# Attention and two mixture layers on one Trainium2 core: a new sequence of product groups, with an offset table for a list scheduler

## The chip, the core and the metric

The kernel runs on one core of a Trainium2 chip. The metric is the device time of one execution in microseconds; a smaller number is better. Times given for a kernel are medians of several executions; a profile shows one execution more. The engines are named TensorE (PE, with its weight loads as PEld), VectorE (DVE), ScalarE (ACT), GpSimd (POOL) and SyncE (SP); DMA engines move data between HBM and the core's SBUF.

## What is computed

Three layers, one behind the other, on 2304 tokens of width 512. All inputs and results are float32.

```python
# q, k, v: (4, 8, 576, 64)
scores = scale * np.matmul(q, k.transpose(0, 1, 3, 2))
rel = pos[:, None] - pos[None, :]
scores = np.where((rel >= 0) & (rel < 64), scores, -1e9)
attn = softmax(scores)                        # (4, 8, 576, 576), a band of 64
x = concat_heads(np.matmul(attn, v))          # (2304, 512)

h = x @ w_in                                  # (512, 2048)
x = (h - np.tanh(h)) @ w_out                  # (2048, 512)

logits = cosine(x, expert_emb) / tau          # (2304, 8)
expert_idx = np.argmax(logits, axis=1)
gate_w = softmax(logits)[arange, expert_idx]
for e in range(8):
    mask = expert_idx == e
    h = np.maximum(x[mask] @ w1[e], 0.0)      # (512, 1024)
    out[mask] = gate_w[mask, None] * (h @ w2[e])
```

## The kernel before

The kernel has a straight part and a routed part. The straight part computes the attention, the dense layer, the routing and most of expert 0, and has no branch. The routed part goes through the experts one by one, with branches on how many tokens each has.

**Precision.** TensorE multiplies fp32r values. A float32 operand is split into a high and a low part, and `mm3` (L607 to L609) issues three matmuls for each product: high x high, high x low, low x high. The split makes much work for VectorE: the weights of the dense layer are decoded by `t_decode` in half-weights, with three bit operations (L375, L381, L386) and one subtraction (L400) on VectorE each, of 128x512 elements.

**Tiles.** Tokens are taken in nine chunks of 256. For each chunk, two units of attention run (`t_attn`: scores L468, masked maximum L484, exponential L493, division L504, transposes L517, product with v L542). The result is the dense layer's input, transposed; it is used directly (`direct`), and for a chunk whose later products come much later it is also stored to HBM (`spill`, L563) and loaded again by `t_xload`.

**The dense layer.** `t_moe1(c, f, ...)` does two of the 16 slices ("halves" f, f+1) of the inner width for chunk c: first products `h<-x,w`, then h - tanh(h), then second products `o<-w,gh`. The elementwise step has four ScalarE operations (square L635, tanh L639, L643, L647), four VectorE operations (L651, L655, L660, L664), a rounding on ScalarE (L670, `gh`) and a subtraction on VectorE (L674). A list `order` gives the sequence of product groups: (chunk, first slice, end slice, where the input comes from). `t_sum` adds the partial sums at a group's end (L706), and stores them to HBM (L711) where the chunk goes on later, or hands them to `t_route` (transposes L768, logits L784, counts L841, L842, prefix sums L850, L860, scatter of list entries L865).

**Routing.** Behind chunk 6's routing, `t_turns` puts the experts in an order by their token counts: counts' matmul L1174, small VectorE operations, cast of the turn L1198, then SP reads the eight numbers into registers (L1228) and loads the first lists (`t_list`, L1268, L1270). VectorE makes row numbers from a list (`t_ids`, L924, L925), and GpSimd gathers the rows with an indirect DMA (`t_gather`, L937). TensorE transposes them (`t_xin`, L960) and multiplies them with the expert's weights (`t_ffn`, loads L903, relu L996, L1000, gated result L1049, L1050, scatter L1055). At the end of the straight part, `t_counts` writes the final counts (L1289); all engines read them (L1375) for the branches (L1413, L1424). The overflow block of an expert, rows 256 to 511 of its list, is gathered too (`blk_o`) and opens the routed part with its transposes (L1070).

**What sets the order.** All work is given as tasks to `Sched`, which runs on the host while the program is built. A task has a priority, dependencies, buffers and a time per engine that can do it. At each step of its own clock the ready task with the lowest priority number, whose engine and buffers are free, is emitted; so these numbers set the sequence of instructions on each engine's queue, and no more. Each queue then runs in that order and waits with semaphores.

```python
later += [t for x in ready for t in (self.ready_at(x[3], e) for e in x[2]) if t > self.now]
...
end = self.moved = max(self.moved, self.now + issue + 0.65) + 1.2 * dur
```

Priorities come from `slot_t`, a table of due times: 3.7 per slice for the first 16 slices and 2.9 for each one behind that.

## Time and profile before

| | |
|---|---|
| median of 3 runs | 814.69 us (813.77 to 815.09) |
| profiled execution, time | 817.42 us |
| its span | 815.7 us |
| mean granted clock of TensorE | 0.989 |
| TensorE busy | 767.8 us (94%) |
| VectorE busy | 592.6 us (73%) |
| ScalarE busy | 475.7 us (58%) |
| GpSimd busy | 91.5 us (11%) |

The profile is of one execution. The span is the time from its first to its last instruction; the rest of the execution's time lies around it. Busy time of an engine is the sum of its instructions without waits. A wait is put down to the instruction that released it. The granted clock is 1.00 for 2.4 GHz and 0.50 for 1.2 GHz.

### The profile page before, as it was taken

The numbers are of one execution on the slowest core, as the hardware profiler recorded it, in microseconds if no ns is written. First come the engines' busy times: TensorE is split into PE (matmuls) and PEld (weight loads), VectorE is DVE, ScalarE is ACT, GpSimd is POOL, SyncE is SP. The second block draws the span as 40 slices with busy tenths as digits, with TensorE's granted clock in tenths as the row PEclk, the third lists the DMA queues.
The fourth block names the chain that finished last, engine by engine and source line by source line (L and its number), as shares of the span: only waits on it lengthen the run. The fifth ranks groups of instructions, "written<-read, shape, count | busy, mean of one in ns | idle before, by whom it ended". The sixth has DMA issues, their size and how long they took to land. (4 is left out here: it accounts for less than half of the span.)

```text
span 815.7 us, 15547 instructions
## 1 busy us (share of the span) xinstructions
PE 767.8 (94%) x5703; PEld 673.5 (83%) x5703; DVE 592.6 (73%) x1492; ACT 475.7 (58%) x1125; POOL 91.5 (11%) x116
## 2 busy tenths in 40 slices
PE   4788999999998999999999799999999999999995
PEld 4676889888987888899898699878888988888894
DVE  6999999999987877866768778983183727714750
ACT  6987888987855676766556456742252424423430
POOL 3000000000011200100001100202021223002320
PEclk9999999999999999999999999999999999999998
DMA  9857655565435342101000342635063728623740
GB/s 301 259 185 226 202 182 167 185 223 198 155 117 98 128 70 94 66 28 51 27 1 27 106 130 75 192 119 152 18 198 106 237 77 277 195 84 101 253 131 23
DMA packets 67438, 111.42 MB, mean 137 GB/s; under 512 B 8580, under 2 KB 44420, under 8 KB 67344
## 3 DMA queue, kind: packets, MB, share of 16 engines
q1 hardware_dynamic: 62448, 97.07, 37.9%
q0 software_dynamic: 4896, 13.13, 5.4%
q8 instruction: 54, 0.88, 0.5%
q14 instruction: 40, 0.33, 0.1%
HBM read 89.57 MB, written 21.66 MB: 136 GB/s over the span
## 5 line engine op out<-in xcount | busy, mean ns | idle before, releaser
L607 PE MATMUL h<-x,w 128*128 128x256 f32 x712 | 205.5, 289 | 4.7 <-DVE g L660 4.6
L608 PE MATMUL h<-x,w 128*128 128x256 f32 x712 | 201.4, 283 | 3.5 <-DVE x L583 3.5
L609 PE MATMUL h<-x,w 128*128 128x256 f32 x712 | 201.5, 283 | 0.9 <-DVE w L400 0.9
L607 PE MATMUL o<-w,gh 128*128 128x512 f32 x436 | 177.6, 407 | 1.0 <-ACT gh L670 0.9
L609 PE MATMUL o<-w,gh 128*128 128x512 f32 x436 | 172.8, 396 | 3.4 <-DVE gh L674 2.7
L608 PE MATMUL o<-w,gh 128*128 128x512 f32 x436 | 172.4, 395 | 0.0
L607 PEld LDWEIGHTS h<-x,w 128*128 128x128 f32 x712 | 135.7, 191 | 12.1 <-issue 5.7
L608 PEld LDWEIGHTS h<-x,w 128*128 128x128 f32 x712 | 136.0, 191 | 6.8 <-DVE x L583 3.9
L609 PEld LDWEIGHTS h<-x,w 128*128 128x128 f32 x712 | 135.9, 191 | 1.3 <-DVE w L400 1.3
L609 PEld LDWEIGHTS o<-w,gh 128*128 128x128 f32 x436 | 82.8, 190 | 26.6 <-DVE gh L674 6.0
L607 PEld LDWEIGHTS o<-w,gh 128*128 128x128 f32 x436 | 83.2, 191 | 19.1 <-issue 2.4
L608 PEld LDWEIGHTS o<-w,gh 128*128 128x128 f32 x436 | 83.3, 191 | 13.3
L888 DVE TENSOR_TENSOR w<-st,w 128x512 fp32r<-128x512 f32 x128 | 83.1, 685 | 3.0 <-ACT w L231 2.4
L231 ACT CAST w<-st 128x512 fp32r<-128x512 f32 x119 | 71.6, 633 | 18.3 <-DMA st<-in_moe_w_dram 8.2
L670 ACT CAST gh<-g 128x512 fp32r<-128x512 f32 x72 | 44.3, 620 | 62.7 <-DVE g L664 58.0
L651 DVE TENSOR_TENSOR g<-h,g 128x512 f32<-128x512 f32 x72 | 49.4, 687 | 25.6 <-ACT g L639 25.1
L996 ACT ACTIVATE gh<-h 128x256 fp32r<-128x256 f32 x48 | 18.1, 383 | 77.7 <-PE h L609 65.4
L674 DVE TENSOR_TENSOR gh<-g,gh 128x512 fp32r<-128x512 f32 x72 | 49.0, 685 | 13.1 <-ACT gh L670 13.1
L493 ACT ACTIVATE pr<-pr,mx 128x128 f32<-128x128 f32 x144 | 56.0, 396 | 3.4 <-DVE mx L484 3.4
L1000 DVE SCALAR_TENSOR_TENSOR gh<-h,gh 128x256 fp32r<-128x256 f32 x48 | 20.0, 421 | 50.6 <-ACT gh L996 43.2
L664 DVE COPY_PREDICATED g<-big,g 128x512 f32<-128x512 uint16 x72 | 53.6, 745 | 3.2
L635 ACT ACTIVATE g<-h 128x512 f32<-128x512 f32 x72 | 42.9, 595 | 19.7 <-PE h L609 19.5
(205 smaller groups left out, 1332.1 us busy)
## 6 DMA issues: line engine op xcount, KB each, us to landing
st<-in_moe_w_dram SPq DMA_DIRECT2D x64, 512.0 KB, 4.7
st<-in_moe_w_in_dram SPq DMA_DIRECT2D x16, 512.0 KB, 5.3
st<-in_moe_w_out_dram SPq DMA_DIRECT2D x16, 512.0 KB, 5.0
v<-in_v_dram SPq DMA_DIRECT2D x16, 512.0 KB
part<-st SPq DMA_DIRECT2D x12, 512.0 KB, 3.0
st<-part SPq DMA_DIRECT2D x12, 512.0 KB, 4.5
k<-in_k_dram SPq DMA_DIRECT2D x16, 320.0 KB, 3.3
q<-in_q_dram SPq DMA_DIRECT2D x18, 256.0 KB, 5.8
```

Source lines behind the costliest of these rows:

```text
L231: return {ACT: (act, lambda: nc.scalar.copy(out=o(), in_=i())), DVE: (dve, lambda: nc.vector.tensor_copy(out=o(), in_=i()))}
L493: nc.scalar.activation(out=pr_.t[:, i, :], in_=pr_.t[:, i, :], func=AF.Exp, bias=st["m"][:, i:i + 1], scale=-1.0, accum_out=st["den"][:, i ...
L607: nc.tensor.matmul(out=ps, lhsT=ah, rhs=bh, start=start, stop=False)
L608: nc.tensor.matmul(out=ps, lhsT=ah, rhs=bl, start=False, stop=False)
L609: nc.tensor.matmul(out=ps, lhsT=al, rhs=bh, start=False, stop=stop)
L635: {ACT: (0.49, lambda: nc.scalar.activation(out=u(), in_=hp.t, func=AF.Square))},
L651: {DVE: (0.6, lambda: nc.vector.tensor_tensor(out=th(), in0=hp.t, in1=th(), op=ALU.subtract))},
L664: {DVE: (0.64, lambda: nc.vector.copy_predicated(out=sq(), mask=big.t.bitcast(DT.uint16), data=th()))},
L670: {ACT: (0.52, lambda: nc.scalar.copy(out=gh(), in_=sq()))}, reads=[(gq, 0), (acc[0], "-"), (acc[1], "-")],
L674: {DVE: (0.6, lambda: nc.vector.tensor_tensor(out=gl(), in0=sq(), in1=gh().bitcast(F32), op=ALU.subtract))},
L888: return lambda: eng.tensor_tensor(out=w.t[:, b], in0=raw.t[:, a], in1=w.t[:, a].bitcast(F32), op=ALU.subtract)
L1000: {DVE: (0.335, lambda: nc.vector.scalar_tensor_tensor(out=part(gs, 1), in0=hp.t[:, 0:CT], scalar=0.0, in1=part(gs, 0).bitcast(F32), op0=A ...
```

## The change

It has three parts, all in what the host-side scheduler is told. No instruction's form changes.

1. *Another sequence of product groups for chunks 0 to 3.* There were 14 groups and are now 13, with other bounds (4, 6, 8, 10, 12, 16 instead of 4, 8, 12, 16). Chunks 0 and 1 now hold their input until their last group; only 2 and 3 are spilled and loaded again.
2. *Costs of transfers.* A transfer's first byte comes 1.0 after its issue instead of 0.65, reading n registers on SP costs 0.6n + 0.1 instead of 0.45, and gathers of the straight part take 1.5 on GpSimd and 3.5 more until they land, instead of 1.04 and 2.0.
3. *A table of 807 offsets.* `SC.part()` stands in front of each group of tasks and takes the next number; a quarter of it is added to the priority of all tasks that follow, until the next call. It acts in the straight part alone.

```diff
+SHIFTS = (
+    -617, -89, -188, -90, -232, 135, -108, -84, -118, -93, -65, -74, -74, -76, 12, -30, -48, -70, 95, -705,
...
+)
-    ISSUE, ISSUE_HALF = 0.45, 0.625
+    ISSUE, ISSUE_HALF, FIRST = 0.45, 0.625, 1.0
+        self.shifts, self.shift = iter(()), 0.0
+    def part(self):
+        self.shift = next(self.shifts, 0) / 4.0
-        self.todo.append((prio, self.n, alts, deps, bufs, list(allocs), lat, before))
+        self.todo.append((prio + self.shift, self.n, alts, deps, bufs, list(allocs), lat, before))
-                dur, fn = alts[e]
+                dur, fn, *own = alts[e]
-                    issue = self.ISSUE_HALF if dur == HALF else self.ISSUE
+                    issue = own[0] if own else self.ISSUE_HALF if dur == HALF else self.ISSUE
-                    end = self.moved = max(self.moved, self.now + issue + 0.65) + 1.2 * dur
+                    end = self.moved = max(self.moved, self.now + issue + self.FIRST) + 1.2 * dur
...
+        SC.part()
         SC.add({DMA: (1.5, load)}, writes=[(raw, 0)], allocs=[raw], prio=pr - 8)
+        SC.part()
         SC.add(
             {ACT: (0.56, d1)}, reads=[(raw, 0)], writes=[(tmp, 0)], allocs=[tmp] + ([w] if o == 0 else []), prio=pr
         )
...
-                {POOL: (1.04, ga)}, reads=[uid, *[("x2d", c) for c in range(chunks)]], writes=[(r[i], 0)],
-                allocs=[r[i]], prio=pr, lat=2.0,
+                {POOL: (took[0], ga)}, reads=[uid, *[("x2d", c) for c in range(chunks)]], writes=[(r[i], 0)],
+                allocs=[r[i]], prio=pr, lat=took[1],
...
-                {DMA: (0.0, lambda i0=i0, i1=i1: regs(i0, i1))}, reads=[("turn", "v")], ...
+                {DMA: (0.0, lambda i0=i0, i1=i1: regs(i0, i1), 0.6 * (i1 - i0) + 0.1)}, reads=[("turn", "v")], ...
...
+    SC.shifts = iter(SHIFTS)
+    FAR = 1.5, 3.5
-    order = [(0, 0, 4, "x"), (1, 0, 4, "x"), (1, 4, 8, ""), (0, 4, 8, ""), (2, 0, 8, "w"), (3, 0, 8, "w"), (1, 8, 12, ""), (0, 8, 12, ""), (2, 8, 12, "load"), (3, 8, 12, "load"), (3, 12, 16, ""), (2, 12, 16, ""), (0, 12, 16, "load"), (1, 12, 16, "load")]
+    order = [(0, 0, 4, 'x'), (1, 0, 6, 'x'), (2, 0, 6, 'w'), (0, 4, 8, ''), (3, 0, 8, 'w'), (2, 6, 10, ''), (1, 6, 10, ''), (0, 8, 12, ''), (3, 8, 12, ''), (1, 10, 16, ''), (0, 12, 16, ''), (2, 10, 16, 'load'), (3, 12, 16, 'load')]
...
     SC.run()
+    SC.shifts, SC.shift = iter(()), 0.0
```

In the sequences below, lines of the change have other numbers: L706 stands for L651 before, L710 for L655, L715 for L660, L719 for L664, L729 for L674, L987 for L924, L1001 for L937, L1125 for L1055, L1451 for L1375.

**VectorE, at the first elementwise step of the dense layer** (chunk 0, slices 0 and 1; L651, L655, L660, L664). Before:

```order
L504 TENSOR_TENSOR pr_367<-pr_367,den 128x512
L651 TENSOR_TENSOR g_541<-h_485,g_541 128x512
L231 COPY pT_547<-a_546 128x512
L655 SCALAR_TENSOR_TENSOR g_542<-g_542,g_540 128x512
L375 TENSOR_SCALAR tmp_581<-tmp_581 128x512
L660 TENSOR_TENSOR g_542<-h_485,g_542 128x512
L381 SCALAR_TENSOR_TENSOR tmp_581<-st_252,tmp_581 128x512
```

With the change:

```order
L534 ISA pr_443,mx<-a_442,mask_84 128x128
L534 ISA mx 128x1
L706 TENSOR_TENSOR g_542<-h_485,g_542 128x512
L710 SCALAR_TENSOR_TENSOR g_543<-g_543,g_541 128x512
L426 SCALAR_TENSOR_TENSOR tmp_519<-st_386,tmp_519 128x512
L715 TENSOR_TENSOR g_543<-h_485,g_543 128x512
L447 TENSOR_TENSOR w_479<-st_348,w_479 128x512
```

The first elementwise operation stands at row 103 of the queue before and at row 110 now; a weight subtraction (L447) and masked maxima are mixed with it where a division and a copy of transposed probabilities were.

**VectorE, between the cast of the experts' turn and the first row numbers of a list.** `pad`, `cum` and `tmp` are small tiles of the padding that `t_turns` computes. Before:

```order
L1198 CAST turni<-turnf 128x8
L660 TENSOR_TENSOR g_5804<-h_5714,g_5804 128x512
L1212 TENSOR_SCALAR pad<-most 128x1 x4
L1216 TENSOR_TENSOR pad<-pad,row_92 128x4
...
L664 COPY_PREDICATED g_5804<-big_5805,g_5803 128x512
L674 TENSOR_TENSOR gh_5980<-g_5804,gh_5980 128x512
L651 TENSOR_TENSOR g_5983<-h_5789,g_5983 128x512
L924 TENSOR_SCALAR gic<-lb 128x2
```

With the change:

```order
L1268 CAST turni<-turnf 128x8
L706 TENSOR_TENSOR g_6083<-h_5972,g_6083 128x512
L710 SCALAR_TENSOR_TENSOR g_6084<-g_6084,g_6082 128x512
L1283 TENSOR_SCALAR pad<-most 128x1 x4
...
L715 TENSOR_TENSOR g_6084<-h_5972,g_6084 128x512
L719 COPY_PREDICATED g_6084<-big_6085,g_6083 128x512
L729 TENSOR_TENSOR gh_6239<-g_5994,gh_6239 128x512
L729 TENSOR_TENSOR gh_6243<-g_6084,gh_6243 128x512
L706 TENSOR_TENSOR g_6264<-h_6048,g_6264 128x512
L710 SCALAR_TENSOR_TENSOR g_6265<-g_6265,g_6263 128x512
L987 TENSOR_SCALAR gic<-lb 128x2
```

Four large operations stand between the cast and the row numbers before, and eight with the change; the padding is there in both.

**GpSimd, at the end of the straight part.** `lst` takes list entries, `g` the rows of overflow blocks and `out_dram` an expert's results. Before:

```order
L865 DMA lst<-pg,su 18432x2 x2
L1375 TENSOR_LOAD cnti
L937 DMA g_7163<-x2d,gic 128x512
L937 DMA g_7185<-x2d,gic 128x512
L1055 DMA out_dram<-pr_7187,idc 2304x512
L1055 DMA out_dram<-pr_7189,idc 2304x512
L1413 COMPARE_AND_BRANCH
```

With the change:

```order
L927 DMA lst<-pg,su 18432x2 x3
L1125 DMA out_dram<-pr_7064,idc 2304x512
L1451 TENSOR_LOAD cnti
L1001 DMA g_7163<-x2d,gic 128x512
L1001 DMA g_7172<-x2d,gic 128x512
L1125 DMA out_dram<-pr_7066,idc 2304x512
L1490 COMPARE_AND_BRANCH
```

One of the two stores of results has moved ahead of the register load and of the two gathers; the branch follows the other one.

## Rows read from the trace of the kernel before

**Rows 1.** The page, engine totals: busy us, share of the span, instructions.

```profile
PE 767.8 (94%) x5703; PEld 673.5 (83%) x5703; DVE 592.6 (73%) x1492; ACT 475.7 (58%) x1125; POOL 91.5 (11%) x116
```

**Rows 2.** Table by stage: length, busy us (count) of PE, PEld, DVE, ACT, POOL, clock, DMA share, GB/s.

```profile
0.00:40.00 40.00, 24.74 (x324) 20.90 (x325) 31.91 (x119) 31.91 (x105) 7.23 (x34) 0.96 0.89 284
40.00:200.00 160.00, 152.17 (x1354) 133.40 (x1354) 158.73 (x396) 135.38 (x333) 0.57 (x1) 0.99 0.62 199
...
250.00:262.00 12.00, 9.95 (x96) 8.44 (x95) 8.29 (x21) 7.15 (x15) 2.46 (x2) 1.00 0.44 96
...
440.00:471.00 31.00, 25.53 (x155) 21.88 (x154) 24.68 (x75) 15.04 (x27) 4.44 (x4) 0.94 0.28 97
...
530.00:562.50 32.50, 30.74 (x197) 25.74 (x196) 21.74 (x69) 10.58 (x25) 5.73 (x6) 1.00 0.30 90
562.50:815.70 253.20, 237.62 (x1401) 207.06 (x1399) 122.48 (x271) 87.35 (x186) 49.17 (x47) 0.99 0.47 147
```

**Rows 3.** The same table for the stretches after two waits of TensorE.

```profile
467.00:470.50 3.50, 3.44 (x10) 2.86 (x11) 3.05 (x5) 1.80 (x4) 0.00 (x0) 0.52 1.02 412
...
461.30:464.40 3.10, 3.10 (x25) 2.94 (x25) 3.06 (x6) 1.86 (x3) 1.21 (x1) 1.00 0.54 107
```

**Rows 4.** Timeline 444 to 468 us: start, length, engine, line, operation, in brackets idle time before.

```profile
444.64 0.18 PE L1174 MATMUL a<-cum,ones 128*128 128x8 bf16 x1
...
452.13 0.17 DVE L1198 CAST turni<-turnf 128x8 int32<-128x8 f32 x1
...
459.06 0.17 DVE L924 TENSOR_SCALAR gic<-lb 128x2 uint32<-128x2 f32 x1 [1.23 <-DMA lb<-lst]
...
461.25 0.36 PE L607 MATMUL h<-x,w 128*128 128x256 f32 x1 [1.79 <-DVE g L660]
...
461.55 1.21 POOL L937 DMA_INDIRECT v<-x2d,gic  x1 [0.30 <-issue]
...
467.06 0.44 PE L960 MATMUL a<-ident,v 128*128 128x128 f32 x1 [2.59 <-DMA v<-x2d,gic]
```

**Rows 5.** Timeline of VectorE, 192 to 197 us.

```profile
192.46 0.67 DVE L651 TENSOR_TENSOR g<-h,g 128x512 f32<-128x512 f32 x1
193.06 0.67 DVE L655 SCALAR_TENSOR_TENSOR g<-g,g 128x512 f32<-128x512 f32 x1
...
196.05 0.67 DVE L674 TENSOR_TENSOR gh<-g,gh 128x512 fp32r<-128x512 f32 x1
```

**Rows 6.** Timeline of TensorE and GpSimd, 548 to 567 us.

```profile
548.13 0.17 PE L842 MATMUL a<-oh,upper 128*128 128x8 bf16 x1
...
556.71 0.28 PE L609 MATMUL h<-x,w 128*128 128x256 f32 x1
556.83 0.40 PE L607 MATMUL o<-w,gh 128*128 128x512 f32 x1
557.07 0.40 PE L608 MATMUL o<-w,gh 128*128 128x512 f32 x1
...
558.62 1.00 POOL L937 DMA_INDIRECT g<-x2d,gic  x1 [7.09 <-DVE gic L924]
559.92 0.97 POOL L937 DMA_INDIRECT g<-x2d,gic  x1 [0.30 <-issue]
...
562.45 0.60 PE L1070 MATMUL a<-ident,g 128*128 128x128 f32 x4
...
566.14 0.50 PE L607 MATMUL a<-w,x 128*128 128x512 f32 x1 [1.22 <-DVE x L1080]
```

**Rows 7.** Timeline of VectorE, 31.5 us.

```profile
31.49 0.69 DVE L651 TENSOR_TENSOR g<-h,g 128x512 f32<-128x512 f32 x1 [1.56 <-ACT g L639]
```

**Rows 8.** Waits of TensorE in 250 to 262 us: total, times, longest.

```profile
PE a L768 <- DVE st L706: 0.9, 1, 0.9
```

**Rows 9.** Line L1508: duration ns min/median/max, first and last start.

```profile
L1508 PEldq COMPARE_BRANCH  x1: 3624/3624/3624, 806.3 to 806.3; - x1
```

**Rows 10.** DMA issues in 458 to 470 us: KB each, us to landing.

```profile
st<-in_moe_w_dram SPq DMA_DIRECT2D x4, 512.0 KB, 6.2
```

More of the change, by code (lines that the diff above doesn't have):

```diff
@@ L451, in t_attn @@
                 alts[POOL] = (1.04, lambda go=go: go(nc.gpsimd))
+            if i != 1:
+                SC.part()
             SC.add(
@@ L471, in s_mm @@
                         )
+        SC.part()
         SC.add(
@@ L527, in t_attn @@
             )
+            SC.part()
             SC.add(
@@ L552, in t_attn @@
             x = xT[c]
+        SC.part()
         SC.add(
@@ L590, in t_xload @@
         t0 = c * CT
+        SC.part()
         SC.add(
@@ L627, in t_moe1 @@
         for i in range(2):
+            SC.part()
             SC.add(
@@ L633, in t_moe1 @@
         u, th, sq = ((lambda b_=b_: b_.t.rearrange("p a b -> p (a b)")) for b_ in (gu, gt, gq))
+        SC.part()
         SC.add(
@@ L687, in t_moe1 @@
         for j in range(2):
+            SC.part()
             SC.add(
@@ L697, in t_sum @@
         if more:
+            SC.part()
             SC.add(
@@ L707, in t_sum @@
                     out=x2.t[:, h], in0=acc[i].t, in1=x2.t[:, h], op=ALU.add))}
+            SC.part()
             SC.add(alts, reads=[(acc[i], 0)], writes=[(x2, i)], allocs=[x2] if i == 0 and not more else [], prio=pr)
         if not last:
+            SC.part()
             SC.add(
@@ L729, in t_route @@
         st = {}
+        SC.part()
         SC.add(
@@ L770, in tr @@
                     )
+            SC.part()
             SC.add({PE: (0.43, tr)}, reads=[(x2, i)], writes=[(ps, 0)], allocs=[ps] + ([xt] if i == 0 else []), prio=pr)
@@ L829, in n3 @@
             nc.vector.tensor_copy(out=st["pg"][:, :, 0], in_=tok[:, 2 * c:2 * c + 2])
+        SC.part()
         SC.add({DVE: (1.23, n1)}, reads=[(at_, 0), ("nrm", c)], writes=[("oh", c)], prio=pr)
@@ L911, in ld @@
                     )
+            SC.part()
             SC.add(
@@ L925, in ids, with t_gather @@
             nc.vector.tensor_copy(out=st["ids"], in_=lb_[:, :, 0])
+        SC.part()
         SC.add({DVE: (0.15, ids)}, reads=[key], writes=[uid], prio=pr)
-    def t_gather(lb_, key, where, pr, chunks=NC, made=None):
+    def t_gather(lb_, key, where, pr, chunks=NC, made=None, took=(1.04, 2.0)):
         r = [Buf(where, hold=True) for _ in range(2)]
@@ L940, in ga @@
                 )
+            SC.part()
             SC.add(
-                {POOL: (1.04, ga)}, reads=[uid, *[("x2d", c) for c in range(chunks)]], writes=[(r[i], 0)],
-                allocs=[r[i]], prio=pr, lat=2.0,
+                {POOL: (took[0], ga)}, reads=[uid, *[("x2d", c) for c in range(chunks)]], writes=[(r[i], 0)],
+                allocs=[r[i]], prio=pr, lat=took[1],
             )
@@ L963, in tr @@
                         )
+            SC.part()
             SC.add(
@@ L988, in t_p1 @@
         wk = [(w, (i, f // 4)) for w in ws[:KD] for i in range(2)]
+        SC.part()
         SC.add({PE: (1.44, p1)}, reads=xk + wk, writes=[(hp, 0)], allocs=allocs, prio=pr, line=line)
@@ L994, in t_relu @@
     def t_relu(hp, gs, pr, allocs=()):
+        SC.part()
         SC.add(
@@ L1032, in t_ffn @@
             w = ws[KD + f // 2]
+            SC.part()
             SC.add(
@@ L1047, in t_out @@
         yt = lambda: rows(y)
+        SC.part()
         SC.add(
@@ L1198, in order_ @@
             nc.vector.tensor_copy(out=turni, in_=turnf)
+        SC.part()
         SC.add({DVE: (1.2, first)}, reads=[(a, 0)], writes=[("turn", "v")], prio=pr)
@@ L1230, in t_turns @@
         for i, (i0, i1) in enumerate(((0, 2), (2, E))):
+            SC.part()
             SC.add(
-                {DMA: (0.0, lambda i0=i0, i1=i1: regs(i0, i1))}, reads=[("turn", "v")], writes=[("turn", i)], prio=pr + 15.0 * i,
+                {DMA: (0.0, lambda i0=i0, i1=i1: regs(i0, i1), 0.6 * (i1 - i0) + 0.1)}, reads=[("turn", "v")], writes=[("turn", i)], prio=pr + 15.0 * i,
                 line="turn",
@@ L1274, in go @@
             after(ld, puts[-2:-1])
+        SC.part()
         SC.add({DMA: (0.1, go)}, reads=[("turn", 0 if i < 2 else 1), ("lst", 0)], writes=[("lb", i, b)], prio=pr)
@@ L1289, in go @@
             nc.vector.tensor_copy(out=cnti, in_=cntp)
+        SC.part()
         SC.add({DVE: (2.6, go)}, reads=[(a, 0)], writes=[("cnt", 0)], prio=pr + 3)
@@ L1364, in attn_moe_moe2 @@
     ws = t_expert(0, lambda j: fin - 40.0 + 2.5 * j)
-    blk = t_gather(lb[:, 0, 0], ("lb", 0, 0), "v", fin - 30.0, NC - 2, listed(0, 0))
+    blk = t_gather(lb[:, 0, 0], ("lb", 0, 0), "v", fin - 30.0, NC - 2, listed(0, 0), FAR)
     x = t_xin(blk, fin - 15.0)
@@ L1369, in attn_moe_moe2 @@
     t_counts(fin)
-    blk_n = t_gather(lb[:, 1, 0], ("lb", 1, 0), "v", fin - 5.0, NC - 2, listed(1, 0))
-    blk_o = t_gather(lb[:, 0, 1], ("lb", 0, 1), "g", fin, made=listed(0, 1))
+    blk_n = t_gather(lb[:, 1, 0], ("lb", 1, 0), "v", fin - 5.0, NC - 2, listed(1, 0), FAR)
+    blk_o = t_gather(lb[:, 0, 1], ("lb", 0, 1), "g", fin, made=listed(0, 1), took=FAR)
     vals = []
```

35 rows, old and new, of the table SHIFTS are left out of this document.

## The prediction

> **What bounds the kernel now.** I read the engine totals first [rows 1]: TensorE is busy 767.8 of 815.7 us, 94%, VectorE 592.6. So the time is TensorE's work plus the 47.9 us in which it stands still, and no edit here removes TensorE work: the change only reorders it. The table by stage [rows 2] says where the idle time is: 15.26 us before 40 us, 7.83 from 40 to 200, 2.05 from 250 to 262, 5.47 from 440 to 471, 1.76 from 530 to 562.5, 15.58 behind that. These six add up to the 47.9 us, so there is none in between. What a stage is worth is what ends its waits. From 40 to 200 us VectorE is busy 158.73 of 160 us [rows 2], so there TensorE waits for VectorE in whatever order VectorE has its work; from 440 to 471 VectorE is free for 6.3 us and the longest wait is for a gather (2.59 us, `v<-x2d`) [rows 4]. The part behind 562.5 us is the routed experts, in which TensorE's order is the same in both kernels, row for row; I leave its 253.2 us alone except for its first wait. The profiled execution took 817.42 us (span 815.7 and 1.72 around it), 2.73 above the median of the runs, 814.69. The sum below is a difference, taken from the median.
>
> A price that recurs is the clock. After TensorE stood still for 2.59 us its granted clock was 0.52 from 467 to 470.5, half speed (1.2 of 2.4 GHz) for nearly all of it; after a wait of 1.79 us it was 1.00 from 461.3 to 464.4 [rows 3, 4]. The stretch behind the gather loses 3.5 x 0.48 = 1.7 us. I charge 1.7 for each wait near or over 2.6 us in a stage that TensorE bounds.
>
> **The early part (term 1).** While VectorE bounds, TensorE's delay at a product is VectorE's work ahead of what the product needs, plus VectorE's idle time, less TensorE's work ahead of the product. I listed VectorE's and TensorE's instructions in both orders up to each product and gave each the step from its start to the next start: 0.60 us for a 128x512 operation on VectorE [rows 5], 0.12 and some 0.23 for a 256-wide and a 512-wide matmul [rows 6], the others likewise. In the kernel before, the largest difference is at the second product of chunk 2, half 8: 185.6 us of VectorE work against 157.8 us of TensorE work, 27.8. The trace agrees: its `gh` (L674) starts at 196.05 [rows 5]; with its step of 0.6 that is 185.6 and 11.1 us of idle time. In the new order the largest is 23.2, at chunk 1, half 8 (160.1 against 136.9): the same 28 half-weights are decoded by then, but more products stand ahead. Gain: 27.8 - 23.2 = 4.6 us. VectorE's own idle time shrinks too. At 31.49 it waited 1.56 us for the first tanh on ScalarE (L639) [rows 7]. In the new order that first operation has 25.4 us of VectorE work ahead of it instead of 22.0, 3.4 more than before, which covers 1.56. Sum -6.2 us. Bounds: -8, if the eight transfers that fall away (four stores of transposed blocks, two reloads, one partial sum stored and reloaded) also free the early queue, in which DMA is 0.89 busy [rows 2]; -2, if VectorE's idle time grows by some 4 us, two or three more stalls like that at 31.49.
>
> **250 to 262 us (term 2).** Three waits, for `gh` and for the sum of a chunk (L706), make 2.05 us [rows 2]; the one for the sum is 0.9 [rows 8]. By the order, the second product that waits there is that of chunk 0, half 14, with 10.9 us of TensorE work between it and its first product; in the new order the pairs at this place have 15.8 us or more. I take -2.0, with 0 (all come back elsewhere) and -2.7 as bounds; the last is by how much TensorE's delay (the time less its work so far) grows from 243 to 260 us, 39.9 to 43.0, less its slow drift.
>
> **440 to 471 us (term 3).** This is a chain through five engines [rows 4]. The counts' matmul (L1174) starts at 444.64; VectorE casts the experts' turn at 452.13; SP reads eight registers and loads the lists; VectorE's ids come at 459.06, having stood 1.23 for the lists; GpSimd issues the second gather until 462.76; TensorE's transposes go on at 467.06, 22.4 us from the start. TensorE had 15.6 us of other work in the span before, and 25.3 in the new order. Behind the waiting ids on VectorE stood `g` work (L655, L660), so TensorE also lost time for `g` products, 1.79 us of it at 461.25 [rows 4]. In the new order eight 512-wide operations (4.8 us) and the padding (1.9) lie between the cast and the ids, 6.7 us against the 6.9 us from the cast to the ids before; the ids wait some 0.2 us. I leave 1.0 us for a product that waits for an `h` bank. So -5.47 (idle, [rows 2]) -1.7 (clock) +1.0 = -6.1 with rounding. Bounds: -7.1, nothing left, and +2, if the gather comes as late as the 4.3 us from its issue's end (462.76 to 467.06) plus delay from the three weight loads that are now issued around it, where four came behind it (four of 512 KB, [rows 10]).
>
> **530 to 545 us (term 4).** The waits here, 1.76 us in sum [rows 2], are for VectorE and ScalarE work that is laid out otherwise now; I take half: -0.8. Bounds -1.7 and +1.
>
> **The end of the straight part (term 5).** In the kernel before, the transposes that open the overflow block of expert 0 (L1070) start at 562.45 with no wait [rows 6]. The chain to them begins at the prefix matmul of the last chunk, 548.13, and goes over the lists and ids to the gathers, issued from 558.62 to 559.62 and from 559.92 to 560.89: the second ends 12.8 us behind the matmul, in which TensorE had 14.3 us of work left. In the new order it has 11.4 us left, and its first transposes read the second gather (g3), behind a store of results that stood behind the gathers. So that gather's issue ends 12.8 - 11.4 = 1.4 us after TensorE has run dry. It lands no later than 2.83 us after its issue for the first one before (559.62 to 562.45) and 4.3 us in [rows 4]; I take 2.2, so TensorE waits 3.5 us and then runs at half clock (1.7). The wait of 1.22 us ahead of 566.14 [rows 6] goes, since the relus it stems from are done while TensorE stands. Sum +4.0. Bounds: 0, if the chain is 5 us faster than I count; +6, for a landing after 4.3.
>
> The branch of expert 0 now follows its own hint directly; before, two products stood between. The dearest branch of TensorE's queue took 3,624 ns, at the program's end [rows 9]; TensorE stands still for the gather as long anyway, so nothing is added. The Trainium skill, "Runtime: NRT & Kernel Launch", Instruction fetch mechanics, speaks against such a hint: a taken branch whose target is not in the window that has been fetched ahead forces a fetch before execution goes on. By that rule the branch could end the wait, not the gather, at 3,624 ns and the load of the register ahead of it, and the sum would be about 1 us higher; that the branch is taken at this place no run shows yet.
>
> **Term 6.** The 807 offsets move nearly every VectorE and ScalarE row by a little. The kernel before has no wait at all in 200 to 250, 262 to 440 and 471 to 530; whether the new order has any there is open. I charge +1, from -1 to +5 (four waits like 1.22).
>
> **Sum:** -6.2 - 2.0 - 6.1 - 0.8 + 4.0 + 1.0 = -10.1. From 814.69 this gives **804.6 us**; the profiled execution would be 807.3.
>
> **Rivals.**
> (a) *The end is covered.* Terms 5 and 6 are 0: the gather comes in time because its lists are ready 5 us earlier than the old chain says. 799.6 us (804.6 - 4.0 - 1.0). For it: of the 10.5 us from the matmul to the first gather [rows 6] part is queueing that another order can drop; against it: the order of POOL.
> (b) *VectorE's early idle time grows.* Its lead is worth nothing if stores and loads arrive late; term 1 is 0: 810.8 us. For it: DMA is 0.89 busy before 40 us [rows 2]. Against: fewer transfers.
> (c) *The gather of expert 0 comes behind the weight loads* (the other side). Place: the transposes that opened at 467.06. Three weight loads are issued around the gather now; a load there took 6.2 us to land [rows 10]. If the gather's rows come behind all three one after another, it is 18.6 us late, less the 2.5 us between landing and use (25.3 less 22.4, less 0.4 for the ids): TensorE stands 16.1 us, 1.7 for the clock, 822.4 us. It decides from about 12.5 us of lateness on, where the wait of 10 eats the whole gain. Against: before, the gathers' rows moved while four loads ran, at 412 GB/s, a share of 1.02 of the engines just behind it [rows 3], and the wait was 2.59. The Trainium skill, "DMA: Bandwidth & Descriptors", Queues, rings and completion order, says that each transfer engine goes round between the queues packet by packet; by that rule the gather shares and doesn't stand behind, the trace agrees, and this rival would fall away.
> (d) *The layout doesn't fit the chip.* The offsets answer to delays that the chip hasn't; many waits under 1 us come in the three stages that have none now, 10 us in sum: 813.6 us.
>
> **How the numbers follow.** Less than 0.2% (1.6 us) can't be told from no change here. Chances: my forecast 0.50 (own range 800.5 to 808), (a) 0.20, (b) 0.17, (c) 0.08, (d) 0.05. (c) and a sliver of (b) and (d) are slower: 0.09. (d) and the tail of (b) make no change: 0.06. The rest, 0.85, is faster. The range 797 to 812 leaves out (c), most of (d) and a few per cent at either end of the others.
>
> **What would show it.** In the profile after: VectorE no longer idle for 1.56 us at its first `g`, and TensorE's idle time before 200 us down from 23.1 us to about 17; no wait over 1 us for `g` or the gather in the stage of the turns, and no stretch at half clock there; a new wait of 3 to 4 us for `g<-x2d`, with half clock behind it, where the straight part ends; 253 us behind it, less 1.2. I am wrong if waits stand in the stages that had none, if TensorE waits over 5 us for any gather, or if the early idle time stays at 23 us.

## The result and the profile after

| | before | after |
|---|---|---|
| median of 6 runs | 815.02 us (813.77 to 818.03) | 805.88 us (803.83 to 808.77) |
| ratio of the two, 95% interval | | 0.9872 (0.9849 to 0.9895) |
| profiled execution, span | 817.42, 815.7 us | 805.82, 804.0 us |
| idle time of TensorE | 47.9 us | 40.4 us |

The change makes the kernel about 9 us faster by the medians (9.1), and 10.4 by the ratio; 804.6 was predicted. The six runs of either kernel spread by 4 to 5 us. The engine totals of the changed kernel answer to [rows 1]:

```profile
PE 763.6 (95%) x5703; PEld 672.4 (84%) x5703; DVE 582.8 (72%) x1482; ACT 472.9 (59%) x1121; POOL 90.9 (11%) x116
```

TensorE is busy 4.2 us less with the same 5703 matmuls; part of that is time that it no longer runs at half clock. The table by stage of the changed kernel, to be read against [rows 2]:

```profile
0.00:40.00 40.00, 24.48 (x331) 20.54 (x331) 33.32 (x129) 32.01 (x103) 6.74 (x33) 1.00 0.83 269
40.00:200.00 160.00, 155.65 (x1447) 136.93 (x1447) 157.41 (x415) 145.61 (x388) 0.94 (x2) 1.00 0.62 200
200.00:262.00 62.00, 62.00 (x546) 54.83 (x545) 54.78 (x149) 41.08 (x101) 4.53 (x4) 1.00 0.44 130
262.00:296.00 34.00, 32.29 (x330) 27.68 (x329) 27.54 (x90) 22.77 (x62) 8.97 (x8) 1.00 0.34 103
...
440.00:471.00 31.00, 31.00 (x219) 28.08 (x218) 23.15 (x64) 17.45 (x32) 2.02 (x2) 1.00 0.05 18
471.00:530.00 59.00, 58.56 (x373) 50.87 (x371) 54.18 (x125) 40.08 (x81) 7.93 (x8) 1.00 0.66 205
530.00:549.80 19.80, 15.58 (x103) 13.37 (x101) 10.97 (x47) 4.02 (x11) 5.90 (x6) 1.00 0.21 55
549.80:804.00 254.20, 240.04 (x1400) 209.97 (x1400) 122.35 (x271) 86.34 (x184) 47.28 (x46) 0.98 0.46 144
```

Between 200 and 262 us and between 440 and 471 us TensorE has no idle time now. From 0 to 200 it has 19.87 us instead of 23.09, and the clock is 1.00 in both rows, where it was 0.96 and 0.99. What is new stands in 262 to 296 (1.71 us), in 471 to 530 (0.44) and, largest, in 530 to 549.8 (4.22 us). Behind 549.8 the routed part takes 254.2 us, 1.0 more than before. Who is waited for, over the whole span:

```profile
PE a L517 <- DMA k<-in_k_dram: 10.0, 2, 6.7
PE a L1140 <- DMA g<-x2d,gic: 3.9, 1, 3.9
PE a L660 <- issue: 2.4, 1, 2.4
PE h L661 <- DVE x L635: 2.0, 1, 2.0
```

No wait for `v<-x2d` is left, and `k` costs what it did (9.7 us before). The largest new one is `g<-x2d`, the gather of the overflow block at the end of the straight part. Its place in the timeline of the changed kernel, GpSimd and TensorE:

```profile
543.29 0.97 POOL L1125 DMA_INDIRECT out_dram<-pr,idc  x1 [5.36 <-ACT pr L1119]
544.72 0.99 POOL L1001 DMA_INDIRECT g<-x2d,gic  x1 [0.46 <-issue]
546.01 0.97 POOL L1001 DMA_INDIRECT g<-x2d,gic  x1 [0.30 <-issue]
...
545.55 0.28 PE L662 MATMUL h<-x,w 128*128 128x256 f32 x1
549.77 0.45 PE L1140 MATMUL a<-ident,g 128*128 128x128 f32 x1 [3.94 <-DMA g<-x2d,gic]
```

The store of results goes first (543.29), then the two gathers; the second, which the transposes read, is issued until 546.98. TensorE runs dry at 545.83 and goes on at 549.77. The stretch behind that wait, and the one behind the wait named "issue" at 673.3, in the table by stretch:

```profile
549.80:553.20 3.40, 3.40 (x17) 3.40 (x18) 0.69 (x1) 0.59 (x1) 0.00 (x0) 0.52 0.92 237
...
675.90:679.30 3.40, 3.40 (x18) 3.40 (x18) 0.43 (x1) 0.63 (x2) 2.51 (x3) 0.50 1.00 361
```

Both run at half clock (0.52 and 0.50), as the stretch behind the gather at 467 us did before [rows 3].

The clock in the early part needs a second look. Before, two stretches ran at half clock there; in the changed kernel's profile none did:

```profile
37.10:40.50 3.40, 2.98 (x9) 2.56 (x10) 3.40 (x7) 2.85 (x8) 0.00 (x0) 0.50 0.79 269
50.70:54.10 3.40, 3.40 (x11) 2.58 (x10) 3.37 (x15) 3.40 (x18) 0.57 (x1) 0.50 0.92 336
```

But clock_fill, a kernel of the experiments below, has the same order of instructions on the four compute engines up to 543 us, and its profile has half clock at 28.4 us, where the changed kernel's has none (first the changed kernel, then clock_fill):

```profile
28.40:31.80 3.40, 3.39 (x28) 3.39 (x29) 3.37 (x15) 2.95 (x9) 0.00 (x0) 1.00 0.99 329
28.40:31.80 3.40, 3.40 (x17) 3.40 (x18) 3.40 (x14) 1.86 (x5) 0.00 (x0) 0.50 0.88 279
```

TensorE had stood still for 2.02 and 1.97 us just before. So with the same order and nearly the same wait the clock fell in one execution and not in the other, and 1.7 us of the difference between two profiles can be that.

### The profile page after: what moved, and what is told of

It is laid out like the page before. It is cut to its first block, busy times and chain, and to the rows that moved or that the text cites. A ratio compares the mean times of both kernels' runs of the same rounds, so it can differ in the third digit from the quotient of the medians.

```text
span 804.0 us, 15561 instructions
## 1 busy us (share of the span) xinstructions
PE 763.6 (95%) x5703; PEld 672.4 (84%) x5703; DVE 582.8 (72%) x1482; ACT 472.9 (59%) x1121; POOL 90.9 (11%) x116
## 5 line engine op out<-in xcount | busy, mean ns | idle before, releaser
L660 PE MATMUL h<-x,w 128*128 128x256 f32 x688 | 198.5, 289 | 1.2 <-DVE g L715 1.1
L661 PE MATMUL h<-x,w 128*128 128x256 f32 x688 | 194.7, 283 | 2.0 <-DVE x L635 2.0
L662 PE MATMUL h<-x,w 128*128 128x256 f32 x688 | 194.6, 283 | 1.4 <-DVE w L447 1.4
L660 PE MATMUL o<-w,gh 128*128 128x512 f32 x436 | 175.2, 402 | 0.0
L662 PE MATMUL o<-w,gh 128*128 128x512 f32 x436 | 171.1, 393 | 0.9 <-DVE gh L729 0.7
L661 PE MATMUL o<-w,gh 128*128 128x512 f32 x436 | 170.9, 392 | 0.0
L660 PEld LDWEIGHTS h<-x,w 128*128 128x128 f32 x688 | 131.4, 191 | 8.2 <-issue 2.6
L661 PEld LDWEIGHTS h<-x,w 128*128 128x128 f32 x688 | 131.5, 191 | 4.8 <-DVE x L635 2.2
L662 PEld LDWEIGHTS h<-x,w 128*128 128x128 f32 x688 | 131.4, 191 | 1.6 <-DVE w L447 1.6
L662 PEld LDWEIGHTS o<-w,gh 128*128 128x128 f32 x436 | 81.9, 188 | 21.4 <-DVE gh L729 2.1
L660 PEld LDWEIGHTS o<-w,gh 128*128 128x128 f32 x436 | 82.2, 188 | 16.4 <-issue 2.0
L661 PEld LDWEIGHTS o<-w,gh 128*128 128x128 f32 x436 | 82.3, 189 | 13.8 <-DVE w L447 0.4
L706 DVE TENSOR_TENSOR g<-h,g 128x512 f32<-128x512 f32 x72 | 49.4, 686 | 29.0 <-ACT g L694 28.9
L729 DVE TENSOR_TENSOR gh<-g,gh 128x512 fp32r<-128x512 f32 x72 | 48.6, 683 | 12.9 <-ACT gh L725 12.8
L698 ACT ACTIVATE g<-g,sqa 128x512 f32<-128x512 f32 x72 | 52.3, 726 | 7.2 <-DVE g L719 4.2
```

Source lines behind the costliest of these rows:

```text
L660: nc.tensor.matmul(out=ps, lhsT=ah, rhs=bh, start=start, stop=False)
L661: nc.tensor.matmul(out=ps, lhsT=ah, rhs=bl, start=False, stop=False)
L662: nc.tensor.matmul(out=ps, lhsT=al, rhs=bh, start=False, stop=stop)
L698: {ACT: (0.62, lambda: nc.scalar.activation(out=sq(), in_=u(), func=AF.Square, scale=SQ_S, bias=sqa))},
L706: {DVE: (0.6, lambda: nc.vector.tensor_tensor(out=th(), in0=hp.t, in1=th(), op=ALU.subtract))},
L729: {DVE: (0.6, lambda: nc.vector.tensor_tensor(out=gl(), in0=sq(), in1=gh().bitcast(F32), op=ALU.subtract))},
```

## The experiments

Theory, as predicted: up to 200 us VectorE's work and idle time set TensorE's delay; behind that the chains of the gathers do; a long wait costs the clock too. The open question is which of the three parts of the change does what.

### The parts of the change

**order_only**: the new sequence of groups alone, the `order` line of the change in the kernel before.

> The kernel before with the new sequence of product groups alone; no table, old costs. Theory (VectorE's lead decides the early part, the gathers' chains the rest): by the order the largest lead of VectorE's work over TensorE's is 29.5 us here against 27.8 before and 23.2 with the whole change, and the chain of the turns has 15.6 us of cover as before. So +1.7 us: about 816.5, from 814 to 819, with the 2.6 us gather wait still there. Rival (the early gain comes from the groups and the spills that fall away): the early part gains about 6 us, about 809.

Measured 811.62 us, ratio 0.9989 (0.9958 to 1.002): no difference that can be told. That is below the expected range by the median, and above the rival's 809. TensorE's idle time before 200 us is 23.4 us in its profile (23.1 before), and the gather's wait stands at 464 us with 2.1. So the groups and the eight transfers that fall away bring by themselves nothing that can be told; the interval leaves room for 3 us and not for the rival's 6. The rise of 1.7 us did not show either; the lead is no finer than that.

**costs_only**: the new costs alone.

```diff
-    end = self.moved = max(self.moved, self.now + issue + 0.65) + 1.2 * dur
+    end = self.moved = max(self.moved, self.now + issue + 1.0) + 1.2 * dur
-    {DMA: (0.0, lambda i0=i0, i1=i1: regs(i0, i1))}
+    {DMA: (0.0, lambda i0=i0, i1=i1: regs(i0, i1), 0.6 * (i1 - i0) + 0.1)}
-    {POOL: (1.04, ga)}, ... lat=2.0
+    {POOL: (1.5, ga)}, ... lat=3.5
```

> The kernel before with the new costs of transfers alone (first byte, register reads, gathers); old groups, no table. Theory: the lead is 28.6 us (+0.8); TensorE has 38.1 us of other work between the counts' matmul of the turns and the first transposes of gathered rows, where it had 15.6 and the chain took 22.4, so the gather wait (2.6), the half clock behind it (1.7) and part of the waits for g ahead of it (2.9) go: 815.0 + 0.8 - 5.5 = about 810, from 808 to 812. The end has 14.3 us of work behind the last prefix matmul as before, so no wait for the overflow gather. Rival (costs alone only shift the wait to another place): 814 to 816.

Measured 806.37 us, ratio 0.9905 (0.9873 to 0.9937): faster than expected, and most of the whole change's gain. The table by stage of this kernel:

```profile
0.00:200.00 200.00, 175.19 (x1677) 152.95 (x1678) 190.57 (x522) 170.89 (x456) 8.21 (x35) 0.98 0.67 214
200.00:262.00 62.00, 62.00 (x484) 55.64 (x482) 54.62 (x127) 41.05 (x92) 7.99 (x7) 1.00 0.44 136
...
440.00:471.00 31.00, 29.92 (x187) 26.22 (x186) 26.81 (x76) 16.58 (x30) 3.13 (x4) 1.00 0.35 120
471.00:552.80 81.80, 80.81 (x530) 71.06 (x529) 65.97 (x154) 45.61 (x92) 11.36 (x11) 1.00 0.37 115
```

The early part is no better (24.8 us idle to 200, 23.1 before). From 200 to 262 the 2.05 us of [rows 2] are gone, which I had not put to the costs; from 440 to 471 1.08 us are left of 5.47, at full clock; and at the end there is no wait for the overflow gather, with 14.3 us of work behind the last prefix matmul as before.

**gather_cost_only**: of the three costs that of the gathers alone.

> The kernel before with the new cost of the straight part's gathers alone (1.5 and 3.5 instead of 1.04 and 2.0). Its lead is 27.8 us as before; between the turns' matmul and the first transposes of gathered rows there are 38.1 us of work as in costs_only. Theory: the gather wait and the clock behind it go, 4.3 us and up to 2.9 of waits for g: 814.7 - 5.5 = about 809, from 807 to 812, with the waits between 250 and 262 us (2.0) still there, since those came from the first-byte cost. Rival (all of the 8 us of costs_only hangs on this one number): 805.5 to 807.

Measured 812.18 us, ratio 0.9973 (0.9953 to 0.9992). The waits of TensorE from 250 to 562 us:

```profile
PE h L623 <- DVE g L678: 2.9, 2, 1.8
PE a L791 <- DVE st L726: 0.9, 1, 0.9
PE o L625 <- DVE gh L692: 0.7, 2, 0.4
```

The gather's wait and its half clock are gone, but 2.9 us for `g` stay, and with them waits of the 250 us stage (L791, `gh`). So the three costs share the gain: this one alone gives 1 to 4 us, and the rest needs the other two; which of the two was not tried, nor what they give without this one.

**no_table**: new groups, new costs, and the table empty (`SHIFTS = ()`).

> The changed kernel with an empty table: new groups and new costs, no offsets. Theory: the largest lead is 43.2 us (at chunk 0, slice 4: 141.0 us of VectorE work against 97.7 of TensorE), 20.0 more than in the changed kernel and 15.4 more than before, so the early part is 15 us slower than before; the gather chain has 38.1 us of cover (-5.5) and the end 14.3 us of work: about 825, from 821 to 829. Rival (the groups and costs carry the gain, the table only polishes): 803 to 810.

Measured 826.59 us, ratio 1.0146 (1.011 to 1.0182), as the lead says. Waits and table by stretch, where the lead grows:

```profile
PE a L530 <- DVE pr L517: 11.9, 4, 5.1
...
60.00:130.00 70.00, 53.92 (x664) 45.63 (x666) 67.36 (x215) 65.46 (x205) 0.00 (x0) 0.88 0.77 240
```

VectorE is busy 67.36 of 70 us, TensorE waits 11.9 us for four divisions (`pr`). One part failed: the overflow gathers were waited for 3.6 us at the end. The first transposes came without a wait, 14.3 us of work behind the last prefix matmul; the wait stands ahead of the second ones, which read the second gather (last section). The table of offsets undoes the lead: on top of groups and costs it is worth 21 us. But costs_only has neither groups nor table, and its interval (0.9873 to 0.9937) overlaps that of the whole change (0.9849 to 0.9895): which of the two is faster these runs can't tell. The table on the old groups was not tried.

### VectorE in the early part

**lead_plus_early**: eight VectorE instructions of the elementwise step issued twice, early. **lead_plus_late**: the same behind 260 us.

```diff
+    TWICE = ((2, 0), (2, 2), (2, 4), (0, 4), (0, 6), (3, 0), (3, 2), (3, 4))     # early
+    TWICE = tuple((5, f) for f in range(0, 16, 2))                               # late
+        def pick():
+            for _ in range(2 if (c, f) in TWICE else 1):
+                nc.vector.copy_predicated(out=sq(), mask=big.t.bitcast(DT.uint16), data=th())
```

> The changed kernel with eight VectorE instructions issued twice (the predicated copy of the elementwise step, which gives the same result the second time), at chunk 2 slices 0 to 4, chunk 0 slices 4 and 6, chunk 3 slices 0 to 4, all ahead of chunk 1 slice 8; the order is otherwise the same. 8 x 0.64 = 5.1 us of VectorE work. Theory (VectorE bounds until 200 us): all of it is added, 805.9 + 5.1 = about 811, from 809 to 813, and TensorE's delay at 190 us is 5 us larger. Rival (VectorE's 98% busy share is no bound, since work could be filled in): 805 to 807.

> The changed kernel with eight predicated copies issued twice as in lead_plus_early, but at chunk 5 (slices 0 to 14), behind 260 us; 5.1 us of VectorE work. Theory (VectorE bounds only until 200 us): VectorE is 72% busy there and TensorE has 7 to 12 us of work between a first and a second product; at most a few tenths of a microsecond at the tightest slices: 805.9 to 807.5. Rival (any VectorE work on a product's path adds to the time): 811, as in lead_plus_early.

Early: 813.23 us, ratio 0.9973 (0.9949 to 0.9996), 7 to 8 us above the changed kernel and just above the expected range. Late: 806.53 us, ratio 0.9913 (0.9884 to 0.9943), within the spread of the changed kernel's. How far TensorE had come by 200 us, in the tables of before, after and early:

```profile
0.00:200.00 200.00, 176.92 (x1677) 154.30 (x1678) 190.65 (x514) 167.30 (x438) 7.80 (x35) 0.98 0.67 216
```
```profile
0.00:200.00 200.00, 180.13 (x1776) 157.47 (x1777) 190.73 (x543) 177.62 (x490) 7.67 (x35) 1.00 0.66 213
```
```profile
0.00:200.00 200.00, 176.50 (x1729) 153.88 (x1729) 190.30 (x527) 171.56 (x468) 8.04 (x35) 0.98 0.63 202
...
113.90:117.30 3.40, 3.40 (x18) 3.40 (x17) 3.40 (x14) 3.24 (x6) 0.00 (x0) 0.50 0.38 151
```

VectorE is busy 190.3 to 190.7 us in all three; TensorE has done 1677, 1776 and 1729 matmuls. So it is bound by how VectorE's 190 us are spent. The 5.1 us cost 7 to 8: one wait grew to 3.96 us, and a stretch at half clock, 1.7 us, came behind it (last row). Late, no wait for `g` or `gh` over 0.3 us appears from 262 to 500 us.

**costs_ta12**: costs_only, and attention units due closer together, which by the order alone gives nearly the lead of the changed kernel, without a table.

```diff
-    TA = 16
+    TA = 12
```

> costs_only with one more number changed: attention units are due every 12 instead of every 16 of the scheduler's units (TA = 12); no table, old groups. Theory (the early part costs VectorE's largest lead): the lead is 24.0 us here (at chunk 0, slice 4) instead of 28.6 in costs_only and 23.2 in the changed kernel, and the late part is that of costs_only: 806.4 - 4.6 = about 802, from 800 to 804.5. Rival (the early gain needs the table's fine placing, or is made of fewer transfers): 805 to 808.

Measured 808.34 us, ratio 0.9928 (0.9905 to 0.995): a miss. Its timeline of VectorE and its table to 200 us show the likely reason:

```profile
94.12 0.69 DVE L692 TENSOR_TENSOR gh<-g,gh 128x512 fp32r<-128x512 f32 x1 [1.84 <-ACT gh L688]
...
0.00:200.00 200.00, 177.64 (x1743) 155.30 (x1744) 187.42 (x523) 171.59 (x474) 7.58 (x35) 0.97 0.67 213
```

VectorE itself stood still for 1.84 us for a `gh` whose product had only just been made, and was busy 187.42 us of 200 instead of 190.7. As I read it, a small lead by the order is worth nothing where VectorE must wait for TensorE to get it: the largest lead came at 66 us of TensorE's work, and the delay was 37 us there already. The lead is a lower bound, to which VectorE's idle time has to be added at the same place.

### The end of the straight part

**table_to_400**: the offsets left out for the last 60 us of the straight part.

```diff
-        self.todo.append((prio + self.shift, self.n, ...
+        self.todo.append((prio + (self.shift if prio < 400 else 0.0), self.n, ...
```

> The changed kernel with the offsets left out for tasks whose own priority is 400 or more, which are the last 60 us of the straight part. Up to 443 us of TensorE work its order is that of the changed kernel. Theory: behind the last prefix matmul there are 15.9 us of TensorE work instead of 11.4, and the chain to the overflow gather needs about 15, so the wait of 3.9 us for it and the half clock behind it go and the 1.2 us wait behind the transposes comes back: 805.9 - 3.9 - 1.7 + 1.2 = about 801.5, from 799.5 to 804. Rival (the wait is for a landing that is slow beside other transfers, whatever the cover): 805 to 807, with a wait of 3 to 4 us for g still there.

Measured 808.2 us, ratio 0.992 (0.9889 to 0.995), above both ranges. The wait for the gather went, as 15.9 us of work behind the last prefix matmul had it; but the waits from 262 us to the end of the straight part are now:

```profile
PE a L845 <- DVE mx L534: 2.6, 1, 2.6
PE a L845 <- ACT w L276: 2.4, 1, 2.4
PE o L662 <- DVE gh L729: 1.1, 2, 0.7
PE a L828 <- DVE st L763: 1.1, 1, 1.1
...
471.00:557.20 86.20, 80.34 (x488) 67.95 (x487) 69.63 (x188) 41.45 (x83) 16.28 (x14) 0.96 0.47 150
```

Waits of 2.4 and 1.1 us come for the routing of the last chunks (`a`, L845 and L828) and 1.1 us for products of the dense layer (`o`). The first row is at 269 us, where the order had not been changed, and was 0.7 in the changed kernel. A clock of 0.96 from 471 to 557 is 6.9 us at half speed (2 x 0.04 x 86.2), which costs 3.4 us. So the table does work there too: without it the wait at the end went, and as much came ahead of it.

**clock_fill**: 24 idle matmuls ahead of the transposes that wait.

```diff
+                def fill():
+                    for d in [*range(KD)] * 2:
+                        t = ws_n[d].t
+                        mm3(dps.t[:, 0:CT], t[:, 2 * P:3 * P], t[:, 1024 + 2 * P:1024 + 3 * P],
+                            x_n.t[:, 0, d, :], x_n.t[:, 1, d, :], d == 0, d == KD - 1)
+                SC.add({PE: (2.88, fill)}, writes=[(dps, 0)], allocs=[dps], prio=t1 - 5.0)
```

> The changed kernel with 24 matmuls of 128x256 (2.88 us) issued ahead of the first transposes of expert 0's overflow block, into a PSUM buffer that nobody reads; they fill most of the 3.9 us wait for the gather. Theory (the half clock behind the wait comes from TensorE standing still): the wait is 1.0 us, the granted clock behind it is 1.0 and 1.7 us are saved: about 804, from 802.5 to 805.5. Rival (the clock falls there for another reason, such as the load on the DMA engines or the kind of matmul): half clock in the same place, 805 to 808.

Measured 797.84 us, ratio 0.9789 (0.9756 to 0.9822): 8 us faster than the changed kernel, where 1.7 was expected. Its timeline and table:

```profile
547.94 0.63 PE L1140 MATMUL a<-ident,g 128*128 128x128 f32 x4 [1.09 <-DMA g<-x2d,gic]
...
547.90:553.00 5.10, 5.06 (x32) 4.61 (x33) 1.38 (x2) 1.18 (x2) 0.00 (x0) 1.00 0.95 377
665.00:690.00 25.00, 25.00 (x165) 22.78 (x164) 18.77 (x40) 10.83 (x23) 6.07 (x6) 1.00 0.73 237
```

The wait is 1.09 us and the clock behind it 1.00, as expected. But TensorE also has no idle time from 665 to 690 us, where the changed kernel had the wait of 2.44 us and its half clock: 4.1 us that I had not seen coming. Between the filled wait and that place the two kernels do the same; what differs is that the code lies 48 places later (24 matmuls and 24 weight loads). With the 1.7 us of the clock that makes 5.8 of the 8 us. The other 2 are not the filling's: TensorE starts its last product of the straight part at 543.7 us instead of 545.6, with the same instructions in the same order on the four compute engines.

**shift_only**: 24 small matmuls at the program's start instead, which move the code too.

```diff
+        for _ in range(24):
+            nc.tensor.matmul(out=wps.t[:, 0:8], lhsT=ident, rhs=ident[:, 0:8], start=True, stop=True)
```

> The changed kernel with 24 matmuls of 8 columns on TensorE ahead of its first work, while it waits 6.6 us for the first k; nobody reads their result. All instructions behind them stand 48 places later in TensorE's code, as those behind the filled wait in clock_fill did. Theory (the wait of 2.4 us that TensorE shows at 673 us behind expert 3's branch, with half clock behind it, is the fetch of code behind a taken branch and hangs on where the code lies): that wait and its half clock go, 4.1 us, and the end of the straight part stays as it was (3.9 us wait, half clock): 805.9 - 4.1 = about 802, from 800 to 803.5. Rival (in clock_fill it went because the work before it came earlier or the clock was up): 2.4 us of wait again, 805 to 807.

Measured 811.65 us, ratio 0.9951 (0.9931 to 0.9971), far above both ranges. The 24 matmuls took 10.4 us, not the 5 that the wait had room for, so all else starts 5.2 us later. The trace also counts 48 matmuls and 48 weight loads for them (L1400), so the code behind lies 96 places later and not the 48 of clock_fill. Their row, and the waits from 550 us on:

```profile
1.42 10.41 PE L1400 MATMUL a<-ident 128*128 128x8 f32 x48 [1.42 <-POOL ident masks.py:199]
...
PE a L1140 <- DMA g<-x2d,gic: 5.8, 1, 5.8
...
PE a L662 <- issue: 1.2, 1, 1.2
```

The wait at 673 us is gone; one of 1.2 us stands behind the branch of a later expert instead (778 us), with no half clock. That part of the theory holds: the wait hangs on where the code lies. That it is the fetch of code is argued; the profile names no cause. The gather's wait is 5.8 us, 1.8 longer; see the last section. 805.9 + 5.2 - 4.1 + 1.2 + 1.8 = 810.0, against 812.5 for the profiled run and 807.4 to 812.5 in all.

**products_ahead**: the two needed products in place of idle matmuls, with the small matmuls still at the start.

```diff
-    for f, at in zip(range(f0, 4), (0.1, 2.5) if f0 else (0.1, 0.2, 2.5, 2.9)):
+    for f, at in zip(range(f0, 4), (-3.0, -2.0) if e == 0 else (0.1, 2.5) if f0 else (0.1, 0.2, 2.5, 2.9)):
```

> shift_only, and the two remaining first products of expert 1, which stood behind the first transposes of expert 0's overflow block and between its later steps, are put ahead of those transposes. They are work that has to be done, so they fill the wait as the idle matmuls of clock_fill did without adding any. Theory: the wait for the gather is 1 us with no half clock behind it (-2.9 - 1.7), and two waits of 1 to 1.4 us come where the products stood: 802 - 4.6 + 2.4 = about 799.5, from 797 to 801.5. Rival (the places behind the transposes need their cover more than the gather's wait does): 801.5 to 804.

Measured 809.61 us, ratio 0.9948 (0.9932 to 0.9964), a miss. The expectation was counted from 802, which did not hold for shift_only. Against that kernel the wait fell from 5.8 to 1.7 us and the half clock went; by the medians it is 2 us faster, by the intervals not clearly.

**ahead_small_fill**: the same products ahead, and the small matmuls in bf16 in front of them.

```diff
+        for _ in range(24):
+            nc.tensor.matmul(out=dps.t[:, 0:8], lhsT=upper, rhs=upper[:, 0:8], start=True, stop=True)
```

> The changed kernel with expert 1's two remaining first products put ahead of the first transposes of the overflow block, as in products_ahead, and 24 matmuls of 8 columns in bf16 (about 0.07 us each, 1.7 us) in front of them instead of at the program's start; so no start is lost and the code behind stands 48 places later as in clock_fill. Theory: 1.7 + 2.9 us of instructions fill the gather's wait, no half clock behind it, no wait at 673 us; 2.9 us of it are needed work, of which two waits of 1.0 and 0.25 us give 1.2 back. Against clock_fill (797.8) about 1.7 us less: 796, from 794.5 to 798.5. Rival (the gather then lands no earlier and the waits that come in the products' place take all back): 798 to 801.

Measured 799.47 us, ratio 0.9815 (0.9786 to 0.9843): faster than the kernel before and the changed one, no faster than clock_fill, and by the median in the rival's range. Its waits from 540 us on:

```profile
PE a L660 <- DVE x L1150: 1.0, 1, 1.0
PE a L661 <- issue: 0.8, 1, 0.8
```

The gather's wait and the "issue" wait at 673 are gone; 1.0 us for `x` came, as expected, and an "issue" wait of 0.8 at 546 us, behind the branch of expert 0. Of the 1.7 us that needed work should save against idle work, the medians show none.

## Why the prediction was right, step by step

- **Term 1 (-6.2).** Right. TensorE's delay when it had 155 to 159 us of its work behind it was 38.2 us before and 32.7 after, 5.5 us less. Its idle time to 200 us fell by 3.2, not by the 6 that I named as the sign; the other part is the half clock of two stretches (at 37 and 51 us), which went too. That part is in no line of the term, and by clock_fill's profile 1.7 us of it can be the execution and not the order: here the term was lucky. lead_plus_early shows the mechanism. But the split into lead and idle time was finer than the measure: order_only and costs_ta12 missed by 2 to 6 us when predicted by the lead alone.
- **Term 2 (-2.0).** Right in size, 2.05 us to none. The reason given, more work between a pair of products in the new sequence, is not the only one: the new costs did the same with the old groups (costs_only, no idle time from 200 to 262).
- **Term 3 (-6.1).** Right. 5.47 us of idle time and 1.7 of half clock became none in 440 to 471 and 0.27 at 476. The turns' matmul is at 464.5 now, the second gather is issued until 483.1, TensorE comes to it at 490.3 without a wait. The 1.0 that I left for an `h` bank is 0.27.
- **Term 4 (-0.8).** Besides the gather's wait 0.28 us are left of 1.76 (4.22 - 3.94), so -1.5.
- **Term 5 (+4.0).** Right: wait 3.94 us (3.5 predicted), half clock behind it, and the 1.22 us wait gone, +4.4. The working holds too: the second gather's issue ended 1.15 us behind the dry point (1.4), and it landed 2.8 us later (2.2). Rival (a) is out for the changed kernel.
- **The branch that follows its hint.** It cost nothing: TensorE's branches of that line took 76 to 469 ns, and the first came at 544.6, before the queue ran dry. It was not taken, since the transposes of its own body (L1140) follow at 549.77. The Trainium skill's rule on taken branches ("Runtime: NRT & Kernel Launch", Instruction fetch mechanics) so did not apply there; it fits the wait at 673 us, which stands behind a branch that jumps (no L1140 stands between it and the next branch of its line) and went when the code moved.
- **Term 6 (+1.0).** Too small. 1.7 us of new waits came in 262 to 296, where there had been none; I had named that as a sign of being wrong. The "issue" wait grew from 1.48 to 2.44 and brought a half clock of 1.7, which no term held; so the part behind 549.8 us is 1.0 longer, where I had put it 1.2 shorter. Together that is +4.4, within the bounds of the term.
- **The sum.** As measured the terms add up to about -7 (-5.5 - 2.05 - 6.9 - 1.5 + 4.4 + 4.4), where -10.1 was predicted and the medians moved by -9.1 (the two profiled executions by -11.6). So term 6 was short by 3.4 us, and about 2 us of gain lie in no term; that 804.6 came within 1.3 us of 805.88 is partly luck.
- **Rivals.** (b): VectorE's idle time did not grow. (c): TensorE did not wait for the gather of expert 0. (d): true of neither kernel as a whole; yet no_table shows that the same groups and costs without the offsets are 21 us slower.

What I could not see before: the three parts are not three gains. The costs alone give about 8 us (5 to 10 by the interval); the new groups with the table add the early 5 to 6, and take back 4.4 at the end, 1.7 in new waits and a longer wait at 673 us.

## What to carry to other kernels

Where a host-side scheduler lays out the queues, correct the times that it takes for transfers, register reads and gathers first: on the old groups three numbers gave as much as the whole change with its 807 offsets, within what the runs can tell. They are no cure by themselves: on the new groups, without offsets, the same three numbers came with 826.59 us. Where one engine bounds a stage, add up its work ahead of each thing that the other waits for, and its own idle time at the same place; one without the other misleads. If a wait of several microseconds on TensorE can't be avoided, put needed work, or even idle matmuls, into it: with 2.88 us of them in a wait of 3.94 the half clock behind it did not come.

## What the runs showed that I had not expected

*The landing of a gather goes with the start of the weight loads.* Where SP's next 512 KB loads were issued 2 us behind the gather, it was there 2.8 us after its issue (546.98 to 549.77 in the changed kernel, loads from 549.12). In lead_plus_late, with the same order, the loads came as the gather's issue ended:

```profile
545.26 0.97 POOL L1005 DMA_INDIRECT g<-x2d,gic  x1 [0.30 <-issue]
...
546.11 2.38 SPq L969 DMA_DIRECT2D st<-in_moe_w_dram  x4
...
550.63 0.66 PE L1144 MATMUL a<-ident,g 128*128 128x128 f32 x2 [5.54 <-DMA g<-x2d,gic]
```

It took 4.4 us (546.24 to 550.63); 4.6 in shift_only, and 7.0 in no_table, where the loads began 0.84 us ahead of the issue's end. Between these lie products_ahead, 3.4 us with the loads 0.18 us behind, and clock_fill, 2.8 with the loads 0.57 us behind. No run changed the start of the loads alone. So rival (c) has a mechanism behind it, at 2 to 4 us instead of 16. The gather does not stand behind all loads. In lead_plus_late it landed ahead of the four loads that were issued beside it, which took 6.7 us in the median (the first was there at 551.4 us); the DMA issues from 545 to 553 us (us from issue to landing last):

```profile
st<-in_moe_w_dram SPq DMA_DIRECT2D x4, 512.0 KB, 6.7
g<-x2d,gic POOLq DMA_INDIRECT x1, 5.2
```

In no_table it landed behind the first load (572.8 us) and ahead of the other three (from 575.1 on). The Trainium skill's rule that the transfer engines go round between queues packet by packet ("DMA: Bandwidth & Descriptors", Queues, rings and completion order) agrees with that: the gather is slowed and shares.

*Code position.* The "issue" wait behind the jump of expert 3's branch was 1.5 to 2.8 us in the ten profiles of kernels without added TensorE instructions, and absent at that place in the four with them. In the two with 48 (clock_fill, ahead_small_fill) no later branch has such a wait; in the two with 96 (shift_only, products_ahead) about 1 us came behind a later branch, at 775 to 780 us. Which places are good stays open.

*Small matmuls are not cheap by their columns.* 24 float32 matmuls of 8 columns took 10.4 us in shift_only, 24 of the same shape in bf16 0.76 us in ahead_small_fill:

```profile
542.85 0.76 PE L1497 MATMUL a<-upper 128*128 128x8 bf16 x24
```

The row is to be read against that of L1400 in shift_only, which counts 48 for the 24. In bf16 one took 0.03 us, less than half of the 0.07 that I had expected.
